# Pooled attention and expert routing: scores on all 128 rows, token ranks by a running sum

## The chip, the core and the metric

The kernel runs on one core of a Trainium2 chip. The core has a matrix engine (TensorE, PE in the profile; its weight loads are listed apart as PEld), a vector engine (VectorE, DVE), an engine for activation functions (ScalarE, ACT), a general-purpose one (GpSimd, POOL) and a queue for synchronisation and transfers (SyncE, SP). Each runs its own list of instructions in order and waits on semaphores for the others. Sixteen DMA engines move data between HBM and the on-chip memory SBUF; TensorE writes its results to PSUM, from where VectorE or ScalarE copies them out.

The metric is the device time of one execution, in microseconds (us), as the median of several runs.

## The reference: what is computed

```python
# q, k, v: (8, 8, 576, 64) float32 -- batch, heads, sequence, head size
k_p = k.reshape(B, H, Sp, 8, D).mean(axis=3)         # Sp = 576 / 8 = 72
v_p = v.reshape(B, H, Sp, 8, D).mean(axis=3)
scores = q @ k_p.T / sqrt(64)                        # 576 x 72 for each head
attn = softmax(scores)
x = (attn @ v_p), heads side by side                 # 4608 tokens x 512

for e in range(8):                                   # experts
    mask = domain_id == e                            # one expert for each token
    out[mask] = relu(x[mask] @ w1[e]) @ w2[e]        # 512 -> 1024 -> 512
```

## The kernel before

**Stages.** Attention comes first, in four pairs of batches. A pair has 16 heads (two batches of eight) and nine blocks of 128 tokens. After it come the experts, one after the other, each on the tokens routed to it. Every expert has room for 640 tokens (`CAP`); tokens beyond that go to an overflow loop at the end, which runs zero or more times (`nblk`).

**One pair of batches.** The loads of q, k and v (`load_pair`, L104) are DMAs issued by GpSimd that turn float32 into float16. All twelve stand in one software queue, in the order k, q, v of a pair. For a pair, `kp_units` pools k by matmuls with the identity (L432), copies the sums out, turns them with TensorE (L440) and copies the result to `kpT`. A head is 64 elements deep, so pooled k fills 64 rows; `kpT` holds it twice, in its lower and in its upper 64 rows. `qt_units` turns q in the same way (L495), in units of eight chunks of two tokens, into `qT`: even tokens lie in its lower 64 rows, odd ones in its upper. `vp_units` pools v (L461, L477).

`sc_unit` (L502) makes the scores of one head. Two matmuls (L515), one for each half of the rows (even and odd tokens), write two PSUM banks of a buffer, and one exponential on ScalarE (L518) takes both to `at`. For heads 46 to 63 two more matmuls (L511, "fill") are issued first: identity times some columns of `qT`, into the part of the PSUM buffer that nobody reads. `av_unit` (L521) multiplies `at` with pooled v for one block of 128 tokens (L535); VectorE divides by the sum of the exponentials (L539, L540) into `x_sb`.

**Order.** What runs when in the attention stage is written by hand: `plan` is a list of (time, unit), where one unit of time is one head's scores, and pair `pr` begins at 16 `pr`. It is sorted and issued in that order, so that TensorE's order is fixed. The scores of a head stand at each whole number; the pooling, turning and av units are spread between them with `put`.

**Writing x and gathering it.** After three av units, three blocks of x go to `x_lin` in HBM by a DMA of SyncE (L554). Those of pairs 0 to 2 are held back: `x_rows` first issues a small DMA that reads the last loaded v (`gate`, L559), and SyncE does not go on before that v is there. From `x_lin` the tokens of an expert are gathered by row numbers (`gather`, L598), a GpSimd DMA. The first three gathers of experts 0 and 1 need only the tokens of pairs 0 to 2. On GpSimd's queue stand, in this order: three gathers for expert 0, its w2, three gathers for expert 1, its w1 and its w2.

**Routing.** Which row of an expert's list a token takes is its rank among the tokens of its expert. The one-hot matrix `oh` (L193) has, for each of 36 columns of 128 tokens, eight entries for the experts. `rank_mm` (L204) makes the ranks on TensorE: one matmul with `Ls`, a strictly triangular matrix, counts inside a column, and 35 matmuls with a matrix of ones add the counts of each column to all later ones (L211). `rank_post` makes ranks, an overflow flag `ovf` and the slot from it. `ovf_mm` (L244) does the same 36 matmuls for the flags, `slot_post` (L253) uses them. The number of overflowing tokens is counted in the expert stage: `count_a` and `count_mm` (L279) in expert 2, with a PSUM buffer of kind `small`, and `count_b` (L281) in expert 3, which reads that buffer first.

**Experts.** `l1_units` is the first layer (L648, eight units), `l2_units` the second (L664, up to five), `turn_units` turns gathered rows (L612). `one(i)` gives the PSUM buffer of a second-layer unit: `small` (two buffers) for two of three, `wide` for the third. `hidden` and `paced` tie the gathers to the progress of the first layer. The output rows are scattered by GpSimd DMAs (L673).

Of the kernel before, what the change touches and what calls it, by code (L numbers as in the profile page):

```python
# [39 lines left out]
def kernel(  # L40
# [70 lines left out]
    with tc.manual_schedule():  # L111
# [5 lines left out]
        for t in xg:  # L117
            nc.vector.memzero(t[:].rearrange("p j d -> p (j d)"))
        kt, vt, qt_ = {}, {}, {}
        kt[0] = load_pair(k, 0, "k")  # L120
# [27 lines left out]
        Ls = rt.tile([128, 128], F16, name="Ls")  # L148
        nc.vector.tensor_scalar(out=Ls[:], in0=iota_f[:], scalar1=col_f[:, 0:1], scalar2=None,
                                op0=ALU.is_gt)  # L150
# [21 lines left out]
        for cc in range(NC_):  # L172
# [3 lines left out]
            if cc >= 4:  # L176
# [16 lines left out]
        oh = rt.tile([128, NCH + 1, E], F16, name="oh")  # L193
        nc.vector.memzero(oh[:, NCH, :])
        nc.vector.tensor_tensor(oh[:, 0:NCH, :], dom[:].unsqueeze(2).to_broadcast([128, NCH, E]),
                                iota_f[:, 0:8].unsqueeze(1).to_broadcast([128, NCH, E]),
                                op=ALU.is_equal)
        blk_h = blk_i = c0 = gap = mrow = mt = nblk_f = nblk_i = nov = nov_f = novp = od = ork = ovf = ovf_h = ovs = pos_h = pos_i = rank = rk = rkv = slot_i = slotf = tmp = None
# [5 lines left out]
        def rank_mm():  # L204
            nonlocal rk
            rk = small()
            nc.tensor.matmul(rk[:, 0:8 * (NCH + 1)], Ls[:], oh[:].rearrange("p c e -> p (c e)"),
                             start=True, stop=False)
            for c in range(NCH - 1):
                c1 = NCH + 1 if c < EPAIR * NC_ else NCH  # L210
                nc.tensor.matmul(rk[:, 8 * (c + 1):8 * c1].rearrange("p (c e) -> p c e", e=E), ones[:],  # L211
                                 oh[:, c, :].unsqueeze(1).to_broadcast([128, c1 - c - 1, E]),
                                 start=False, stop=(c == NCH - 2))

        def rank_post():
            nonlocal c0, gap, ovf, ovf_h, rank, rkv, slotf, tmp
            rkv = rk[:, 0:8 * NCH].rearrange("p (c e) -> p c e", e=E)

            gap = rt.tile([128, E], F32, name="gap")
            nc.vector.memzero(gap[:])  # L220
            nc.vector.tensor_scalar(out=gap[:, 0:NEARLY], in0=rk[:, 8 * NCH:8 * NCH + NEARLY],
                                    scalar1=-1.0, scalar2=float(EARLY), op0=ALU.mult, op1=ALU.add)
            nc.vector.tensor_scalar(out=gap[:, 0:NEARLY], in0=gap[:, 0:NEARLY], scalar1=0.0,
                                    scalar2=None, op0=ALU.max)
            tmp = rt.tile([128, NCH, E], F32, name="tmp")
            c0 = EPAIR * NC_
            nc.vector.tensor_copy(tmp[:, 0:c0], rkv[:, 0:c0])
            nc.vector.tensor_tensor(tmp[:, c0:NCH], rkv[:, c0:NCH],
                                    gap[:].unsqueeze(1).to_broadcast([128, NCH - c0, E]), op=ALU.add)
            nc.vector.tensor_tensor(tmp[:], tmp[:], oh[:, 0:NCH, :], op=ALU.mult)  # L230
            rank = const.tile([128, NCH], F32, name="rank")
            nc.vector.tensor_reduce(out=rank[:], in_=tmp[:], op=ALU.add, axis=AX.X)
            ovf = const.tile([128, NCH], F32, name="ovf")
            nc.vector.tensor_scalar(out=ovf[:], in0=rank[:], scalar1=float(CAP), scalar2=None,
                                    op0=ALU.is_ge)
            slotf = rt.tile([128, NCH], F32, name="slotf")
            nc.vector.tensor_scalar(out=slotf[:], in0=dom[:], scalar1=float(CAP), scalar2=None,
                                    op0=ALU.mult)
            nc.vector.tensor_tensor(slotf[:], slotf[:], rank[:], op=ALU.add)

            ovf_h = rt.tile([128, NCH], F16, name="ovf_h")
            nc.vector.tensor_copy(ovf_h[:], ovf[:])

        def ovf_mm():  # L244
            nonlocal ork
            ork = small()
            nc.tensor.matmul(ork[:, 0:NCH], Ls[:], ovf_h[:], start=True, stop=False)
            for c in range(NCH - 1):
                nc.tensor.matmul(ork[:, c + 1:NCH], ones[:],
                                 ovf_h[:, c:c + 1].to_broadcast([128, NCH - 1 - c]),  # L250
                                 start=False, stop=(c == NCH - 2))

        def slot_post():  # L253
            nonlocal od, slot_i

            od = const.tile([128, NCH], F32, name="od")
            nc.vector.tensor_scalar(out=od[:], in0=ork[:, 0:NCH], scalar1=float(NBLK * 128),
                                    scalar2=None, op0=ALU.add)
            nc.vector.tensor_tensor(od[:], od[:], slotf[:], op=ALU.subtract)
            nc.vector.tensor_tensor(od[:], od[:], ovf[:], op=ALU.mult)  # L260
            nc.vector.tensor_tensor(od[:], od[:], slotf[:], op=ALU.add)
            slot_i = const.tile([128, NCH], I32, name="slot_i")
            nc.vector.tensor_copy(slot_i[:], od[:])

        def count_a():
            nonlocal nov, ovs
            v = Later()

            nov = const.tile([128, 2], F16, name="nov")
            ovs = const.tile([128, 1], F32, name="ovs")  # L270
            v.tensor_reduce(out=ovs[:], in_=ovf[:], op=ALU.add, axis=AX.X)
            v.tensor_copy(nov[:, 0:1], ovs[:])
            v.tensor_copy(nov[:, 1:2], ovs[:])
            return v.units

        def count_mm():
            nonlocal novp
            novp = small()
            nc.tensor.matmul(novp[:, 0:2], ones[:], nov[:], start=True, stop=True)  # L279

        def count_b():  # L281
            nonlocal mrow, mt, nblk_f, nblk_i, nov_f
            v = Later()
            nov_f = const.tile([128, 1], F32, name="nov_f")
            v.tensor_copy(nov_f[:], novp[:, 0:1])
# [127 lines left out]
        def kp_units(pr):  # L413
# [3 lines left out]
            kpT = wk.tile([128, 16, 72], F16, tag="kpT", bufs=2, name="kpT")  # L417
# [3 lines left out]
            def evac(dst, src):  # L421
                if pr == 0:
                    nc.scalar.activation(dst, src, AFT.Copy)
                else:
                    nc.vector.tensor_copy(dst, src)

            def pool(w0, w1, t0):
                if t0 == 0:
                    box[w0] = small()
                pv = box[w0][:, 0:64 * (w1 - w0)].rearrange("p (w d) -> p w d", d=64)  # L430
                for t in range(t0, t0 + 4):
                    nc.tensor.matmul(pv, ident[:], kk[:, t, w0:w1, :], start=(t == 0), stop=(t == 7))  # L432
                if t0 == 4:
                    evac(kps[:, w0:w1, :], pv)

            def turn(w0, w1):
                p = small16()
                for w in range(w0, w1):
                    for half in range(2):
                        nc.tensor.transpose(p[64 * half:64 * half + 64, w - w0, :], kps[:, w, :], ident[:])  # L440
                evac(kpT[:].rearrange("p b (w g) -> p w b g", g=8)[:, w0:w1],
                     p[:, 0:w1 - w0, :].rearrange("p w (b g) -> p w b g", g=8))
# [43 lines left out]
        def qt_units(pr):  # L486
# [5 lines left out]
            def unit(j0, n, i):  # L492
# [3 lines left out]
                if i == 1 or (pr == 0 and i == 3):  # L496
                    nc.scalar.activation(qT[:, j0:j0 + n, :], p[:, 0:n, :], AFT.Copy)  # L497
                else:
                    nc.vector.tensor_copy(qT[:, j0:j0 + n, :], p[:, 0:n, :])  # L499
            return [lambda i=i: unit(8 * i, 8 if i < 4 else 4, i) for i in range(5)]  # L500

        def sc_unit(pr, bh, fill):  # L502
# [5 lines left out]
            for par in range(2):  # L508
                if fill:

                    nc.tensor.matmul(p[:, par, 288:512], ident[:],  # L511
                                     s["qT"][:, 0:2, :].rearrange("p a b -> p (a b)")[:, 0:224],
                                     start=True, stop=True, skip_group_check=True)
            for par in range(2):
                nc.tensor.matmul(p[0:72, par, 0:288], s["kpT"][64 * par:64 * par + 64, bh, :],  # L515
                                 s["qT"][64 * par:64 * par + 64, :, 8 * bh:8 * bh + 8],
                                 start=True, stop=True)
# [183 lines left out]
        for pr in range(NP):  # L701
            t0 = 16.0 * pr
            for h in range(16):
                plan.append((t0 + h, -1, lambda pr=pr, h=h: sc_unit(pr, h, 16 * pr + h >= 46)))
# [82 lines left out]
        for e in range(2, E):  # L787
# [6 lines left out]
            run(merge(u, count_a() + [count_mm] if e == 2 else count_b() if e == 3 else []))  # L794
# [120 lines left out]
```

## Time and profile before

| | |
|---|---|
| median of 14 runs | 257.42 us (256.56 to 259.58) |
| profiled execution | 256.22 us |
| its span in the profile | 254.5 us |
| TensorE busy | 228.3 us (90% of the span) |
| VectorE busy | 122.9 us (48%) |
| ScalarE busy | 92.4 us (36%) |
| GpSimd busy | 117.2 us (46%) |
| moved by DMA | 50.22 MB, 197 GB/s on average |
| first score matmul / last | 19.9 us / 89.9 us |

A busy TensorE is not TensorE at its peak: matmuls overlap one another, and the end of one is modelled. The profile names instructions by engine and line. L515, for instance, is the line of the score matmuls; "64\*72 64x288" says that the stationary matrix has 64 rows and 72 columns and that 288 columns of 64 rows stream past it. The page gives the span in 40 slices of 6.36 us; a digit is the busy share of a slice in tenths, and in the row PEclk the share of full speed that TensorE's clock was granted.

### The profile page before, as it was taken

To read this page: it belongs to the slowest core of one execution; us is meant where nothing else is said; L and a number is where in the kernel's file an instruction comes from. 1 tells how busy PE (TensorE), PEld (TensorE's weight loads), DVE (VectorE), ACT (ScalarE), POOL (GpSimd) and SP (SyncE) were. 2 spreads that over 40 slices of the span, in tenths; PEclk is the share of its full clock that TensorE was granted. 3 is DMA by queue.
4 is the path that set the end of the run, shared out by engine and by line. 5 is a ranking of instruction groups with operands and counts; after the bars stand their busy time and mean duration, and the time that the engine had idled before them with its cause. 6 is when DMAs were issued, how large, how long until landed. Compare 5 with 4: busy or idle time off the path is not lost.

```text
span 254.5 us, 5101 instructions
## 1 busy us (share of the span) xinstructions
PE 228.3 (90%) x2084; PEld 145.7 (57%) x2084; DVE 122.9 (48%) x280; ACT 92.4 (36%) x153; POOL 117.2 (46%) x157
## 2 busy tenths in 40 slices
PE   0687989999998979889989989999999999999990
PEld 0565666676666545456745745756755656656640
DVE  7356499697788662324433333532343332343320
ACT  2056747877775726132312301312302312303210
POOL 8001423030000382386846665676676767653042
PEclk9997799999999988999999999999999999999997
DMA  5999999999999299999989969949979969942032
GB/s 101 210 219 214 219 214 217 217 216 213 216 252 405 84 177 236 237 279 183 180 254 199 229 176 206 248 139 160 247 210 194 248 160 201 247 176 106 0 112 92
DMA packets 21373, 50.22 MB, mean 197 GB/s; under 512 B 2334, under 2 KB 10592, under 8 KB 19938
## 3 DMA queue, kind: packets, MB, share of 16 engines
q0 software_dynamic: 19536, 45.10, 83.3%
q1 hardware_dynamic: 1810, 4.76, 4.8%
q8 instruction: 17, 0.28, 0.4%
q14 instruction: 10, 0.08, 0.1%
HBM read 67.15 MB, written 15.20 MB: 324 GB/s over the span
## 4 chain that ended last, share of the span: by engine, by line
PE 53%; DMA 19%; issue 10%; DVE 7%; POOL 6%; ACT 2%; POOLq 1%; DVEq 0%
PE big L648 14%; PE small L664 14%; DMA v<-in_v_dram 7%; DMA v<-in_moe_w_dram 5%; DMA xg<-x_lin,xrow 5%; PE wide L648 5%; PE small L461 4%; POOL out_dram L673 4%; PE wide L664 3%; PE big L515 2%; DVE x_sb L540 2%; PE turn L612 2%; DVE qT L499 2%; PE small L432 2%; POOL xg L598 2%
## 5 line engine op out<-in xcount | busy, mean ns | idle before, releaser
L598 POOL DMA_INDIRECT xg<-x_lin,xrow x40 | 41.5, 1038 | 48.3 <-DVE rcp L539 32.3
L673 POOL DMA_INDIRECT out_dram<-y,tok x40 | 40.3, 1006 | 44.6 <-ACT y L671 18.4
L664 PEld LDWEIGHTS <-hT 128*128 128x128 f16 x272 | 25.9, 98 | 28.2 <-issue 1.6
L518 ACT ACTIVATE at<-big 72x576 f16<-72x576 f32 x45 | 28.7, 644 | 13.0 <-PE big L515 12.3
L654 DVE TENSOR_SCALAR hT<-big 128x640 f16<-128x640 f32 (+1 forms) x24 | 17.4, 724 | 31.9 <-PE big L648 25.7
L671 ACT ACTIVATE y<-small 128x512 f32<-128x512 f32 x16 | 9.6, 597 | 52.7 <-PE small L664 49.8
L652 ACT ACTIVATE hT<-big 128x640 f16<-128x640 f32 (+1 forms) x24 | 15.0, 623 | 32.1 <-PE big L648 32.1
L669 DVE COPY y<-small 128x512 f32<-128x512 f32 x16 | 11.1, 691 | 28.4 <-PE small L664 27.5
L648 PEld LDWEIGHTS <-v 128*128 128x128 f16 x192 | 18.7, 98 | 9.9 <-DMA v<-in_moe_w_dram 2.2
L648 PEld LDWEIGHTS <-k 128*128 128x128 f16 x192 | 18.9, 99 | 8.7 <-issue 1.4
L613 DVE COPY xT<-turn 128x1024 f16<-128x1024 f16 (+1 forms) x24 | 14.3, 597 | 19.1 <-PE turn L612 19.1
L648 PE MATMUL big<-xT,v 128*128 128x320 f16 (+2 forms) x144 | 21.6, 299 | 1.7 <-DMA v<-in_moe_w_dram 1.7
L648 PE MATMUL big<-xT,k 128*128 128x320 f16 (+2 forms) x140 | 21.6, 304 | 0.0
L664 PE MATMUL small<-q,hT 128*128 128x512 f16 x80 | 18.6, 379 | 0.0
L664 PE MATMUL small<-k,hT 128*128 128x512 f16 x80 | 18.4, 379 | 0.0
L664 PE MATMUL small<-v,hT 128*128 128x512 f16 x64 | 14.9, 379 | 1.2 <-DVE y L669 0.8
L535 PEld LDWEIGHTS <-at 72*128 72x128 f16 (+1 forms) x320 | 13.2, 102 | 4.8 <-ACT at L518 0.7
L515 PE MATMUL big<-qT,kpT 64*72 64x288 f16 x90 | 14.5, 318 | 1.3 <-ACT qT L497 0.8
L540 DVE TENSOR_TENSOR x_sb<-big,rcp 128x512 f16<-128x512 f32 x22 | 15.2, 691 | 0.8
L648 PEld LDWEIGHTS <-q 128*128 128x128 f16 x128 | 12.4, 98 | 5.2
L612 PEld LDWEIGHTS <-xg 128*128 128x128 f16 x160 | 10.6, 98 | 7.8 <-DMA xg<-x_lin,xrow 2.8
L612 PE MATMUL turn<-ident,xg 128*128 128x128 f16 x160 | 13.1, 219 | 1.9 <-DMA xg<-x_lin,xrow 1.9
(156 smaller groups left out, 340.1 us busy)
## 6 DMA issues: line engine op xcount, KB each, us to landing
k<-in_moe_w_dram POOLq DMA_DIRECT2D x6, 1024.0 KB, 11.7
q<-in_moe_w_dram POOLq DMA_DIRECT2D x5, 1024.0 KB, 10.9
v<-in_moe_w_dram POOLq DMA_DIRECT2D x5, 1024.0 KB, 11.5
k<-in_k_dram POOLq DMA_DIRECT2D x4, 1152.0 KB, 24.7
v<-in_v_dram POOLq DMA_DIRECT2D x4, 1152.0 KB, 26.2
x_lin<-x_sb SPq DMA_DIRECT2D x12, 384.0 KB, 6.7
q<-in_q_dram POOLq DMA_DIRECT2D x3, 1152.0 KB, 27.0
q<-in_q_dram POOLq DMA_DIRECT2D x1, 768.0 KB, 12.0
```

The costliest lines, as they stand in the source:

```text
L515: nc.tensor.matmul(p[0:72, par, 0:288], s["kpT"][64 * par:64 * par + 64, bh, :], s["qT"][64 * par:64 * par + 64, :, 8 * bh:8 * bh + 8], st ...
L518: nc.scalar.activation(at[0:72, bh % 8, :].rearrange("p (a c) -> p a c", a=2), p[0:72, :, 0:288], AFT.Exp, scale=1.0 / 64.0)
L535: nc.tensor.matmul(pv[r0:r0 + z - a, h, 0:65], s["at", bt][0:72, h, a:z], s["vp"][0:72, 8 * bt + h, :], start=True, stop=True, skip_group_ ...
L540: nc.vector.tensor_tensor(out=x_sb.rearrange("p (h d) -> p h d", d=D), in0=pv[:, :, 0:64], in1=rcp[:].unsqueeze(2).to_broadcast([128, 8, D ...
L598: i = nc.gpsimd.indirect_dma_start(out=xg[e % 2][:, j, :], out_offset=None, in_=x_lin[0:rows, :], in_offset=bass.IndirectOffsetOnAxis(ap=x ...
L612: nc.tensor.transpose(p[:, j - a, kk, :], xg[e % 2][:, j, 128 * kk:128 * kk + 128], ident[:])
L613: nc.vector.tensor_copy(xts[e][:, :, 128 * a:128 * z].rearrange("p k (j c) -> p j k c", c=128), p[:, 0:z - a])
L648: nc.tensor.matmul(p[:, a, 0:m], w1[:, kk, 128 * fi:128 * fi + 128], xT[:, kk, s0 + m * a:s0 + m * a + m], start=(kk == 0), stop=(kk == 3))
L652: nc.scalar.activation(dst, p[:, 0:nh, 0:m], AFT.Relu)
L654: nc.vector.tensor_scalar(out=dst, in0=p[:, 0:nh, 0:m], scalar1=0.0, scalar2=None, op0=ALU.max)
L664: nc.tensor.matmul(p, hT[:, fi, 128 * j:128 * j + 128], w2[:, fi, :], start=(fi == 0), stop=(fi == 7))
L673: i = nc.gpsimd.indirect_dma_start(out=out, out_offset=bass.IndirectOffsetOnAxis(ap=orig[0][:, bl:bl + 1], axis=0), in_=y[:], in_offset=No ...
```

## The change

There are four parts.

1. *Scores on 128 rows.* `kpT` is replaced by `kz`, two fixed buffers that hold a pair's pooled k twice: in the first half the lower 64 rows are filled, in the second the upper 64, and the other rows are zero. They are zeroed once, at the start, by VectorE. A score matmul now takes all 128 rows of `kz` and of `qT`. The copy into it is made in two halves, the lower one by VectorE and the upper one by ScalarE, in every pair (before, ScalarE made the whole copy in pair 0 and VectorE in the others). The fill matmuls are gone.
2. *Ranks.* `Ls` becomes `Lm`, minus one on and below the diagonal. One matmul with it and one with ones give, for each column and expert, minus the number of tokens from this row on and the column's total. A running sum along the columns (`tensor_tensor_scan`, with `cut` to start anew for each expert) turns the totals into counts up to and including each column; the two are added. `oh` is now ordered by expert, then column. The flags' ranks are made the same way.
3. *Count.* The last element of the flags' running sum is the number of overflowing tokens. `count_a`, `count_mm` and `count_b` become one `count`, only on VectorE, in expert 2.
4. *q of pair 0.* The last 12 chunks are turned as 6 and 6 instead of 8 and 4; ScalarE copies the fifth unit instead of the fourth.

```diff
+        kz = [wk.tile([128, 2, 16, 72], F16, tag="kz", bufs=2, name="kz") for i in range(2)]
+        for t in kz:
+            nc.vector.memzero(t[:].rearrange("p a b c -> p (a b c)"))
         kt[0] = load_pair(k, 0, "k")
...
-        Ls = rt.tile([128, 128], F16, name="Ls")
-        nc.vector.tensor_scalar(out=Ls[:], in0=iota_f[:], scalar1=col_f[:, 0:1], scalar2=None,
-                                op0=ALU.is_gt)
+        Lm = rt.tile([128, 128], F16, name="Lm")
+        nc.vector.tensor_scalar(out=Lm[:], in0=iota_f[:], scalar1=col_f[:, 0:1], scalar2=-1.0,
+                                op0=ALU.is_le, op1=ALU.mult)
+        cut = rt.tile([128, E, NCH], F32, name="cut")
+        nc.vector.memset(cut[:], 1.0)
+        nc.vector.memset(cut[:, :, 0:1], 0.0)
...
         def rank_mm():
-            rk = small()
-            nc.tensor.matmul(rk[:, 0:8 * (NCH + 1)], Ls[:], oh[:].rearrange("p c e -> p (c e)"),
-                             start=True, stop=False)
-            for c in range(NCH - 1):
-                c1 = NCH + 1 if c < EPAIR * NC_ else NCH
-                nc.tensor.matmul(rk[:, 8 * (c + 1):8 * c1].rearrange("p (c e) -> p c e", e=E), ones[:],
-                                 oh[:, c, :].unsqueeze(1).to_broadcast([128, c1 - c - 1, E]),
-                                 start=False, stop=(c == NCH - 2))
+            rk = small(), small()
+            for t, w in zip(rk, (Lm, ones)):
+                nc.tensor.matmul(t[:, 0:E * NCH], w[:], oh[:].rearrange("p e c -> p (e c)"),
+                                 start=True, stop=True)
...
+            run_ = rt.tile([128, E, NCH], F32, name="run_")
+            nc.vector.tensor_tensor_scan(run_[:].rearrange("p e c -> p (e c)"),
+                                         cut[:].rearrange("p e c -> p (e c)"), rk[1][:, 0:E * NCH], 0.0,
+                                         op0=ALU.mult, op1=ALU.add)
...
         def ovf_mm():
-            nc.tensor.matmul(ork[:, 0:NCH], Ls[:], ovf_h[:], start=True, stop=False)
-            for c in range(NCH - 1):
-                nc.tensor.matmul(ork[:, c + 1:NCH], ones[:],
-                                 ovf_h[:, c:c + 1].to_broadcast([128, NCH - 1 - c]),
-                                 start=False, stop=(c == NCH - 2))
+            for i, w in enumerate((Lm, ones)):
+                nc.tensor.matmul(ork[:, NCH * i:NCH * i + NCH], w[:], ovf_h[:], start=True, stop=True,
+                                 skip_group_check=True)
         def slot_post():
+            orun = rt.tile([128, NCH], F32, name="orun")
+            nc.vector.tensor_tensor_scan(orun[:], cut[:, 0, :], ork[:, NCH:2 * NCH], 0.0,
+                                         op0=ALU.mult, op1=ALU.add)
+            nov_f = const.tile([128, 1], F32, name="nov_f")
+            nc.vector.tensor_copy(nov_f[:], orun[:, NCH - 1:NCH])
...
-        def count_mm():
-            novp = small()
-            nc.tensor.matmul(novp[:, 0:2], ones[:], nov[:], start=True, stop=True)
-        def count_b():
-            v.tensor_copy(nov_f[:], novp[:, 0:1])
...
-            kpT = wk.tile([128, 16, 72], F16, tag="kpT", bufs=2, name="kpT")
+            kpT = kz[pr % 2]
...
-                evac(kpT[:].rearrange("p b (w g) -> p w b g", g=8)[:, w0:w1],
-                     p[:, 0:w1 - w0, :].rearrange("p w (b g) -> p w b g", g=8))
+                for i, act in ((0, False), (1, True)):
+                    q = slice(64 * i, 64 * i + 64)
+                    evac(kpT[q, i].rearrange("p b (w g) -> p w b g", g=8)[:, w0:w1],
+                         p[q, 0:w1 - w0, :].rearrange("p w (b g) -> p w b g", g=8), act)
...
-                if i == 1 or (pr == 0 and i == 3):
+                if i == 1 or (pr == 0 and i == 4):
...
-            return [lambda i=i: unit(8 * i, 8 if i < 4 else 4, i) for i in range(5)]
+            if pr == 0:
+                cuts = (0, 8, 16, 24, 30, 36)
+            else:
+                cuts = (0, 8, 16, 24, 32, 36)
+            return [lambda i=i: unit(cuts[i], cuts[i + 1] - cuts[i], i) for i in range(5)]
...
-                if fill:
-                    nc.tensor.matmul(p[:, par, 288:512], ident[:],
-                                     s["qT"][:, 0:2, :].rearrange("p a b -> p (a b)")[:, 0:224],
-                                     start=True, stop=True, skip_group_check=True)
-            for par in range(2):
-                nc.tensor.matmul(p[0:72, par, 0:288], s["kpT"][64 * par:64 * par + 64, bh, :],
-                                 s["qT"][64 * par:64 * par + 64, :, 8 * bh:8 * bh + 8],
-                                 start=True, stop=True)
+                nc.tensor.matmul(p[0:72, par, 0:288], s["kpT"][:, par, bh, :],
+                                 s["qT"][:, :, 8 * bh:8 * bh + 8], start=True, stop=True)
...
-            run(merge(u, count_a() + [count_mm] if e == 2 else count_b() if e == 3 else []))
+            run(merge(u, count() if e == 2 else []))
```

## The prediction

> **What bounds the kernel now.** I read the page's slices first, then the chain of waits, then the windows around the places that the chain names, and last the order of instructions on TensorE there. The page:
>
> ```profile
> PE   0687989999998979889989989999999999999990
> ...
> PEclk9997799999999988999999999999999999999997
> DMA  5999999999999299999989969949979969942032
> ```
>
> TensorE and the DMA engines are both full nearly everywhere, so the question is which is late at which point. DMA has one real hole, slice 13 (83 to 89 us), and it is free after 220 us. The chain, in order of time (start, duration, what):
>
> ```profile
> 4.59 17.69 DMA v<-in_v_dram
> ...
> 81.43 3.94 DMA x_lin<-x_sb
> ...
> 95.05 13.88 DMA v<-in_moe_w_dram
> ...
> 120.62 10.10 DMA xg<-x_lin,xrow
> ...
> 146.13 1.74 PE small L664 x8
> ...
> 157.44 2.17 PE big L648 x16
> ...
> 166.14 3.45 PE small L664 x16
> ...
> 175.89 2.17 PE big L648 x16
> ```
>
> Up to 131 us the long steps are DMA: the first v load (until 22.3), the last x write of pair 2 (until 85.4), the w1 load of expert 1 (until 108.9), a gather (until 130.8). From there on it is matmul after matmul.
>
> The attention stage between the first two is TensorE running behind the loads. The twelve q/k/v loads stand in one queue and land one after the other. Adding issue time and time to landing of the DMA view gives k1 27.1, q1 32.7, v1 38.1, k2 44.5, q2 50.0, v2 55.4, k3 60.9, q3 66.4, v3 71.8 us: one each 5.5 us, whatever TensorE does. The last, issued at 46.76:
>
> ```profile
> v<-in_v_dram POOLq DMA_DIRECT2D x1, 1152.0 KB, 25.0
> ```
>
> First uses by TensorE are 30.1, 36.1, 42.6, 48.3, 52.9, 59.5, 65.1, 69.7 and 75.5 us. So TensorE runs 2.9 to 4.5 us behind DMA, 3.7 at v3, and **no saving on TensorE can pull this stage forward by more than that**. The x writes start only when v3 is in (the gate row, at 71.8 us). From there DMA is full again until the last x write is nearly out (window, busy us and count of each engine, clock, DMA share, GB/s):
>
> ```profile
> 83.00:84.00 1.00, 1.00 (x14) 0.55 (x15) 0.86 (x2) 0.65 (x1) 0.00 (x0) 1.00 0.59 237
> 84.00:85.00 1.00, 1.00 (x10) 0.44 (x8) 0.65 (x3) 0.89 (x2) 0.00 (x0) 1.00 0.15 47
> ```
>
> The rows from 72 to 83 all have a share of 0.97 to 1.15.
>
> **Scores.** Before, two 64-row matmuls run side by side in the two halves of the array; after, two 128-row matmuls run one behind the other. The timeline shows what surrounds a pair:
>
> ```profile
> 42.03 0.43 PE L535 MATMUL wide<-vp,at 72*128 72x65 f16 x8
> ...
> 42.39 0.31 PE L515 MATMUL big<-qT,kpT 64*72 64x288 f16 x2
> ...
> 42.97 0.31 PE L515 MATMUL big<-qT,kpT 64*72 64x288 f16 x2
> ...
> 43.21 0.40 PE L461 MATMUL small<-ident,v 128*128 128x128 f16 x4
> ...
> 43.49 0.43 PE L535 MATMUL wide<-vp,at 72*128 72x65 f16 x8
> ...
> 43.76 0.61 PE L461 MATMUL small<-ident,v 128*128 128x128 f16 x8
> ```
>
> Eight av matmuls followed by full-array work take 43.49 to 43.76, 0.27 us; followed by a score pair, 42.03 to 42.39, 0.36. Entering the pair costs 0.09. From the pair's start to the next start it is 42.97 to 43.21, 0.24. A pair thus holds TensorE for 0.33 us. Its columns explain 0.12: the pooling matmuls of 320 columns (L432) follow each other at about 0.135, so 288 columns take 0.12. The rest is the change of mode. After: 2 x 0.12 = 0.24, and nothing on entry or exit if the weight loads hide, as they do for the av matmuls (eight loads and matmuls in 0.27). I take 0.24, a saving of 0.09. Bounds: 0.46, if neither load hides (106 ns each in their row), to 0.24.
>
> Here a rule speaks against the change. The Trainium skill, TensorEngine Tiling (Array Packing), Theoretical Speedup, gives up to twice the speed for a contraction of at most 64 rows; by it each pair loses 0.12, 64 pairs +7.7 us of TensorE. The same page, Key Properties, says that a change of tiling mode, not of tile, drains the engine. Here almost every pair stands alone between full-array work, and the row charges the drains with 0.21 of 0.33 us. I take the row: 64 x 0.09 = 5.8 us less, except that the five pairs at half clock (22.3 to 28.8 us) gain nothing.
>
> The fills (L511) of heads 46 to 63 go too. Fill to pair is 84.00 to 84.30 and pair to next fill 84.30 to 84.55 in the timeline, 0.54 a head, against 0.24 after: 0.30 x 18 = 5.4 us.
>
> How much arrives? Up to v3's first use 38 pairs at full clock save 38 x 0.09 = 3.4 and three filled ones 0.9: 4.3, where DMA allows 3.7. ScalarE gives some back: of each kpT copy one half moves to it while VectorE's half costs what the whole did (0.49 and 0.41; lanes are parallel), so VectorE gains nothing and ScalarE gets about 1.2 us (its own kpT row in pair 0, x2) in each of pairs 1 to 3. It is busy for about 13 of 16.8 us a pair; queued behind are exponentials (0.65), and TensorE waits for their PSUM. I leave 2.5 to 3.7 us at v3. Five more fills (1.5 us) go before the last av of pair 2, so its x_sb is ready at 76 to 78 instead of 81.4.
>
> There DMA takes over. If that write is queued by 80, the 0.59 + 0.15 us left after 83.0 are finished at 83.75; traffic ended somewhere in 84.2 to 85.0 before and landing was 85.37, so landing comes at 84.1 to 84.9: **1.0 us** (0.5 to 1.3). POOL's three gathers, w2 of expert 0, three gathers and w1 of expert 1 follow back to back from 86.4 and move with it. Next, the first x write of pair 3 (issued at 89.06, 0.98 us of DMA at 400 GB/s) falls into the hole, since its av runs 4 to 5 us earlier: another **1.0 us** (0 to 1.5) off the stream, which is saturated from 90 to 131 (shares 0.98 to 1.18), so w1 of expert 1 and the gather at 130.77 come 2.0 earlier. TensorE idles 1.68 us before 108.98 and 1.25 before 130.77, so it can follow.
>
> Now TensorE will stand still some 4 us before the first gather (attention done near 85, landing near 89.4). The clock row first: after the idle 91.9 to 94 the clock fell to half until about 97, and after the thin stretch before 22.3 it was 0.50 until 28.8. The Trainium skill, TensorE: Matmul & The Clock Gate, Part 1, has an idle window of about 3.4 us halve it, until a busy one. By the row 3 us cold are paid already; by the rule, a stop of 4 us makes it two windows, 1.7 us more in expert 0. Its work from 89.4 is 0.45 + 0.25 (turns) + 1.9 (five av) + 5.2 (L648) + 5.2 + 0.7 (L664 and turns) = 13.7 us, with 6.8 us cold +3.4: done at 106.5, still ahead of w1 at 106.9. I charge nothing.
>
> **Counting the overflow.** This part is small in the diff and lies where TensorE alone is the bound. count_mm takes one of the two `small` PSUM buffers at 144.86, and it is read only in the next expert:
>
> ```profile
> 148.64 1.89 PE L664 MATMUL small<-v,hT 128*128 128x512 f16 x8 [0.78 <-DVE y L669]
> ...
> 158.09 0.15 DVE L100 COPY nov_f<-small 128x1 f32<-128x1 f32 x1
> ```
>
> With one buffer left, expert 2's second layer waits for its own copies. By the chain rows above it takes 146.13 to 157.44, 11.31 us; expert 3's 166.14 to 175.89, 9.75. After, nov_f comes from the running sum and no buffer is held: **1.56 us**, with the matmul 1.6. Nine VectorE operations of about 0.17 us in expert 2 instead of 3 and 7 lie beside matmuls (VectorE is under 40% busy). Weights of expert 4 land some 10 us before use.
>
> **Start.** Rank: 36 matmuls, 8.78 to 12.8, become two (0.41 and 0.12): -3.5. Overflow rank: 1.0 to 0.2. Added on VectorE ahead of them: two zeroings of 1152 words, 1.12 x 1152/1280 = 1.0 each, and `cut` about 0.25, so the one-hot is done near 11.0 instead of 8.7. No row shows the running sum; nearest is the 288-element TENSOR_TENSOR at 0.46, at best that, at worst twice: 0.9. Net, the pooling of k starts about 1.1 us earlier (k landed at 10.4), and slot_post 0.8 on top. All of it ends in the wait for v at 22.32, which grows from 0.74 to about 2.7 us: **0**. Without that cover it would be 1.9. The split q chunks (12 as 6+6 instead of 8+4, a copy of about 0.8 on ScalarE starting later) are within 0.2 either way under the same wait.
>
> **Sum.** 1.0 + 1.0 + 1.6 = 3.6 us. The profiled execution took 256.22 (span 254.5 and 1.7 around it): 252.6. The median of the runs is 1.2 above it: 257.42 - 3.6 = **253.8 us**, likely 252.3 to 255.2.
>
> **Rivals.**
> *DMA hides the whole front* (0.18): landing at 85.4 as before because the writes drain late, or ScalarE's extra copies eat the lead. Only the count stays: 257.4 - 1.6 = 255.8. For it: the share near 1 up to 83. Against: the hole after it.
> *TensorE's saving gets through* (0.12): w1 of expert 1 no longer binds and expert 0's end does: gathers moved by 1.2 and no cold stretch give 104.5 instead of 108.98, 4.4 in front, 6.0 in all: 251.4. Against: w1 is DMA-bound.
> *The weight loads of the padded pairs don't hide* (0.08): 0.46 a pair, 0.13 more than now. Until the last av of pair 2, 43 pairs lose 5.6, eight filled ones gain 8 x 0.08 = 0.6: x_sb at 86.4, landing 2.1 later (the fastest x write) at 88.5, 3.1 late; less 1.6, 258.9. It decides from about 0.45 a pair. For it: the two loads alternate with no third buffer in sight. Against: the hidden loads of the av rows.
> *Without fills the clock halves in pair 3 and stays so through expert 0* (0.05): past 17 us cold after 89.4 the start of expert 1 slips over 111.8 and eats the count's gain; wholly cold it gives about 260. Against: padded pairs are full-array work.
>
> **Numbers.** Forecast 0.57, the rivals as above. What a measurement tells from no change is about 0.3%, 0.8 us. Faster by more: forecast, the third way, and most of the hidden front, 0.82; within: 0.09; slower: 0.09. The range 251.5 to 257.2 leaves out the slower cases and the end of the best.
>
> **What would show it.** L515 with 128 rows and 0.24 from start to next start; no idle before it. v3's first use near 72 to 73; last x write landing near 84.4; w1 of expert 1 used near 107; gather before expert 2 near 128.8. Expert 2's second layer at 9.75. The wait for v at 22.3 unchanged in time. I am wrong if v3 is used no earlier than 75, or if the x write lands early and w1 does not.

## The result and the profile after

| | before | after |
|---|---|---|
| median | 257.13 us (47 runs, 255.87 to 259.58) | 255.02 us (10 runs, 253.44 to 255.64) |
| profiled execution, span | 256.22, 254.5 us | 254.80, 253.1 us |
| TensorE, VectorE, ScalarE busy | 228.3, 122.9, 92.4 us | 219.6, 126.3, 94.5 us |

The ratio is 0.9907, with a 95% interval of 0.9882 to 0.9932: 2.1 us faster by the medians, 1.4 by the two profiled executions, where 3.6 were forecast. Here and below a median is over all runs, while a ratio leaves out the few executions that were over 1.5% slower than the fastest of the same kernel. The slices of the page, in tenths:

```profile
PE   0287779998987769989979999999999999999990
...
PEclk9999999999999977999999999999999999999999
DMA  5999999999999389999979979969969959942032
```

TensorE has lost 8.7 us of work, and its row shows it: in the attention stage (up to slice 13) 7s stand where 8s and 9s stood. The DMA row has not moved. The chain of waits of the changed kernel (start, duration, what), at the places where the prediction read it before:

```profile
80.64 4.90 DMA x_lin<-x_sb
...
87.94 3.58 DMA xg<-x_lin,xrow
...
95.21 13.64 DMA v<-in_moe_w_dram
108.90 1.47 PE big L639 x8
...
120.54 10.62 DMA xg<-x_lin,xrow
...
146.48 3.45 PE small L655 x16
...
156.23 2.17 PE big L639 x16
```

The last x write of pair 2 starts 0.8 us earlier and lands at 85.54, 0.2 later than before. Expert 1 starts at 108.90 (108.98 before), and the gather for expert 2, forecast to end 2.0 us earlier, ends at 131.2, 0.4 later than before. Then comes the count: expert 2's second layer takes 146.48 to 156.23, 9.75 us in place of 11.31. Less what the late gather took, expert 3 starts 1.21 us earlier than before. Nearly all of the span's 1.4 us is there. The stages in front, from which 2.0 us were forecast, show nothing.

The scores themselves are as forecast. Two pairs of the changed kernel's timeline, one behind the other:

```profile
82.37 0.42 PE L507 MATMUL big<-qT,kz 128*72 128x288 f16 x2
82.62 0.41 PE L507 MATMUL wide<-qT,kz 128*72 128x288 f16 x2
```

From start to next start it is 0.25 us, with 128 rows. Entering a pair from eight av matmuls costs nothing more:

```profile
46.87 0.43 PE L526 MATMUL big<-vp,at 72*128 72x65 f16 x8
47.14 0.41 PE L507 MATMUL wide<-qT,kz 128*72 128x288 f16 x2
```

That is 0.27 us, where it was 0.36 ahead of a 64-row pair. What reached v3 is another matter: it is first used at 75.42, before at 75.48.

### The profile page after: what moved, and what is told of

Read it like the earlier page. It is cut to its first block, busy times and chain, and to the rows that moved or that the text cites. A ratio compares the mean times of both kernels' runs of the same rounds, so it can differ in the third digit from the quotient of the medians.

```text
span 253.1 us, 4896 instructions
## 1 busy us (share of the span) xinstructions
PE 219.6 (87%) x1979; PEld 146.1 (58%) x1979; DVE 126.3 (50%) x283; ACT 94.5 (37%) x159; POOL 117.2 (46%) x157
## 4 chain that ended last, share of the span: by engine, by line
PE 49%; DMA 13%; DVE 13%; issue 10%; ACT 7%; POOL 5%; POOLq 1%; DVEq 0%; ACTq 0%
PE big L639 14%; PE small L655 14%; DMA xg<-x_lin,xrow 6%; DMA v<-in_moe_w_dram 5%; PE wide L639 5%; ACT at L509 4%; POOL out_dram L664 4%; PE wide L655 3%; DVE x_sb L531 3%; PE small L424 3%; PE turn L603 2%; DVE qT L493 2%; DMA x_lin<-x_sb 2%; PE small L489 2%; PE big L507 2%
## 5 line engine op out<-in xcount | busy, mean ns | idle before, releaser
L507 PE MATMUL big<-qT,kz 128*72 128x288 f16 x90 | 18.3, 287 | 2.5 <-DVE qT L493 1.1
L526 PEld LDWEIGHTS <-at 72*128 72x128 f16 (+1 forms) x320 | 14.8, 104 | 5.9 <-issue 2.6
```

The costliest lines, as they stand in the source:

```text
L507: nc.tensor.matmul(p[0:72, par, 0:288], s["kpT"][:, par, bh, :], s["qT"][:, :, 8 * bh:8 * bh + 8], start=True, stop=True)
L526: nc.tensor.matmul(pv[r0:r0 + z - a, h, 0:65], s["at", bt][0:72, h, a:z], s["vp"][0:72, 8 * bt + h, :], start=True, stop=True, skip_group_ ...
```

## The experiments

Each ratio is to the kernel before, run on the same chip in the same set. The intervals are some 0.3% to either side, so that two kernels are told apart only where they differ by about half a per cent. No run leaves out any part of the computation; where a run adds matmuls to keep TensorE warm, nobody reads their results.

### One part at a time

**The count alone.** The kernel before, with one more column in the overflow matmuls, whose value is the number of overflowing tokens.

```diff
-            for c in range(NCH - 1):
-                nc.tensor.matmul(ork[:, c + 1:NCH], ones[:],
...
+            for c in range(NCH):
+                nc.tensor.matmul(ork[:, c + 1:NCH + 1], ones[:],
...
+            nc.vector.tensor_copy(nov_f[:], ork[:, NCH:NCH + 1])
...
-            run(merge(u, count_a() + [count_mm] if e == 2 else count_b() if e == 3 else []))
+            run(merge(u, count() if e == 2 else []))
```

> The kernel before with only the count changed: the overflow matmuls get one more column and one more matmul, whose result is the number of overflowing tokens; no PSUM buffer is held from expert 2 to expert 3. Theory (the count gives the whole gain, the front is bound by DMA): the second layer of expert 2 takes 9.75 us as in the changed kernel instead of 11.31, and the ratio to before is 0.990 to 0.994, that of the full change within its interval. Rival (scores and ranks bring part of it): the same 9.75 us, but the full change stays ahead of this kernel by 0.5 us or more.

Measured: 0.9939 (0.9910 to 0.9969), 256.23 us where the kernel before took 257.69. Its chain of waits around expert 2's second layer:

```profile
145.86 3.45 PE small L648 x16
...
155.61 2.17 PE big L632 x16
```

9.75 us again. In the kernel before, TensorE stood for 1.24 of the 11.31 us, in two waits for copies that free the other `small` buffer; in the changed kernel it stands for nothing there. So the PSUM buffer held by the count accounts for the 1.56: 1.24 in the waits, and 0.3 in longer matmul records around them.

**All but the count.** The changed kernel with `count_a`, `count_mm` and `count_b` of before.

```diff
-            run(merge(u, count() if e == 2 else []))
+            run(merge(u, count_a() + [count_mm] if e == 2 else count_b() if e == 3 else []))
```

> The changed kernel with the count of before put back (two column sums, a matmul into a held PSUM buffer, its reading in expert 3). Theory (count only): expert 2's second layer at about 11.3 us again and the ratio to before within 0.002 of 1. Rival (front brings part): ratio 0.996 to 0.998, about 0.7 us of gain left.

Measured: 0.9963 (0.9942 to 0.9984), 256.53 us. Expert 2's second layer takes 11.30 us (146.85 to 158.15), and both waits are back:

```profile
149.34 1.89 PE L670 MATMUL small<-v,hT 128*128 128x512 f16 x8 [0.78 <-DVE y L675]
...
156.26 1.89 PE L670 MATMUL small<-v,hT 128*128 128x512 f16 x8 [0.46 <-ACT y L677]
```

The interval leaves out 1, as the rival had it: a little is left without the count, 0.2 to 0.6%.

**Scores undone.** The changed kernel with `kpT`, its undivided copy, 64-row pairs and fills. With `kz` the two zeroings at the start go too.

```diff
-                nc.tensor.matmul(p[0:72, par, 0:288], s["kpT"][:, par, bh, :],
-                                 s["qT"][:, :, 8 * bh:8 * bh + 8], start=True, stop=True)
+                nc.tensor.matmul(p[0:72, par, 0:288], s["kpT"][64 * par:64 * par + 64, bh, :],
+                                 s["qT"][64 * par:64 * par + 64, :, 8 * bh:8 * bh + 8],
...
```

> The changed kernel with the score part put back: 64-row pairs side by side, fills for heads 46 to 63, one undivided copy of turned k. Theory (front bound by DMA): same time as the full change within 0.3 us, w1 of expert 1 used near 108.9 us as in both kernels. Rival (padding brings part): slower than the full change by 0.7 us. Rival (padding costs, by its divided copies): faster than the full change by 0.5 us or more.

Measured: 0.9924 (0.9894 to 0.9954), 256.24 us, which cannot be told from the changed kernel. v3 is first used at 72.68, **2.7 us earlier** than with the padded scores, and expert 1 starts at 108.08. Nearly all of the 2.7 us is there at the first score already (19.60 instead of 22.23): it is the zeroings that are missing, not the padding.

**Ranks undone.** The changed kernel with the 36 rank matmuls of before, and the count from the extra column.

```diff
-            for t, w in zip(rk, (Lm, ones)):
...
+            for c in range(NCH - 1):
...
+                nc.tensor.matmul(rk[:, 8 * (c + 1):8 * c1].rearrange("p (c e) -> p c e", e=E), ones[:],
...
```

> The changed scores, count and q chunks with the 36 rank matmuls of before. Theory (these matmuls raised TensorE's clock ahead of the pooling of k): the 16 pooling matmuls of pair 0 take 2.1 us as before instead of 4.0, the first scores start before v lands, at 20 to 21 us instead of 22.2, and the end moves by less than 0.3 us since DMA decides it. Rival (the pooling took 4.0 us because of PSUM buffers held by the ranks, not of the clock): the single pooling matmuls keep their distance of 0.13 us in the changed kernel but wait once in the middle; undoing the ranks then also gives 2.1 us.

Measured: 0.9947 (0.9921 to 0.9973), 256.38 us. The pooling of k takes 2.60 us. That the first score would come at 20 to 21 us was a miss: it comes at 23.42, since the 36 matmuls themselves take 4.60 us behind the zeroings, and v3 at 77.22.

**The changed kernel and the count alone, side by side,** five rounds each:

> The changed kernel again, unedited, beside the next run on the same chip. Theory (the stages ahead of the experts bring a little through pair 2's last av and the start of expert 1): ratio to the kernel before 0.990 to 0.992, and 0.2 to 0.4% (0.5 to 1.0 us) below the kernel that has the new count alone. Rival (only the count is worth anything): the two ratios lie within 0.15% of each other.

> The kernel before with the new count alone, again. Theory: ratio 0.993 to 0.995, so that 0.2 to 0.4% of the change's gain is left to the padded scores. Rival: the same ratio as the changed kernel within 0.15%, and the padded scores bring nothing that can be measured.

Measured: the changed kernel 0.9934 (0.9908 to 0.9960), 255.25 us; the count alone 0.9922 (0.9900 to 0.9945), 255.44 us. The rival holds: **side by side, nothing beyond the count can be measured.** The changed kernel without the count, 0.4% faster with an interval that leaves out 1, speaks for a small rest. Between nothing and 0.6% it stays open.

### Does it matter when attention is done?

Every run has its own first use of v3, so the profiles together answer this. Ten of fourteen follow; the other four have v3 at 74.8 to 74.9 us and the first gather at 86.1 to 86.7. The columns are starts in us: the first score, v3's first use, the first gather, GpSimd's issue of expert 1's w1 where the chain names it, and the start of expert 1.

| kernel | first score | v3 used | first gather | w1 issued | expert 1 |
|---|---|---|---|---|---|
| scores undone | 19.60 | 72.68 | 86.41 | - | 108.08 |
| count alone | 20.70 | 73.59 | 86.10 | 94.79 | 108.43 |
| warm start (below) | 20.39 | 73.79 | 86.76 | 95.41 | 108.41 |
| count alone, again | 21.01 | 73.89 | 86.65 | 95.31 | 109.41 |
| copies by buffer (below) | 22.21 | 74.75 | 86.46 | 95.13 | 108.79 |
| changed kernel | 22.23 | 75.42 | 86.55 | 95.21 | 108.90 |
| before | 19.92 | 75.48 | 86.38 | 95.05 | 108.98 |
| changed kernel, again | 22.33 | 75.52 | 86.38 | 95.04 | 108.47 |
| ranks undone | 23.42 | 77.22 | 86.05 | - | 109.99 |
| three edits (below) | 25.94 | 78.48 | 87.03 | 95.70 | 110.58 |

v3's first use moves over 5.8 us, the first gather over 1.0, and not in step with it. From there to w1's issue it is 8.65 to 8.69 us in every row that has both. So an earlier end of attention buys nothing at the gathers. For the start of expert 1, one profile tells little below 1 us: the count alone has 108.43 and 109.41. But a late end costs: with v3 after 77, expert 1 starts at 110.0 and 110.6, behind all the others of the table. Why the gather stays shows in the windows of the changed kernel (window, busy us and count of PE, PEld, DVE, ACT and POOL, clock, DMA share, GB/s):

```profile
83.00:84.00 1.00, 0.82 (x11) 0.54 (x10) 0.64 (x4) 1.00 (x3) 0.00 (x0) 1.00 0.69 273
84.00:85.00 1.00, 0.80 (x11) 0.52 (x10) 0.89 (x2) 1.00 (x3) 0.00 (x0) 1.00 0.14 55
```

Before, these rows had 0.59 and 0.15. The same traffic is still on its way, although x was ready sooner. The write that is ready earlier waits in the DMA engines: ready at 79.49 with the warm start it landed after 6.26 us, ready at 81.43 before after 3.94. TensorE does not set when this traffic begins. The gate on v3 does, at 71.80 us before and here at

```profile
71.97 0.31 SPq L550 DMA_DIRECT2D gate<-v  x1
```

and from 72 to 83 us the DMA share of the changed kernel is 0.99 to 1.13 in every row.

### Where the padded scores' lead went

The row of v3 above splits in two. The first score is 2.31 us later than before, and the stretch from there to v3 is 53.19 us instead of 55.56. But with the count alone, with 64-row pairs, that stretch is 52.88: the kernel before ran at half clock from 22.0 to 28.8 us, which no other profile here shows (in its runs of the later sets the mean granted clock is 0.977 to 0.980, that of the changed kernel 0.976 to 0.979). With only the scores undone it is 53.08. At full clock the padded pairs bring the stretch nothing. TensorE's busy time in it is less (47.09 us, against 48.51 with the scores undone and 49.23 with the count alone), and its waits are as much longer. The waits of the changed kernel in this stretch (who waits for whom: us, times, longest) name the new ones:

```profile
ACT kz L415 <- DVE kz L417: 2.9, 6, 0.9
...
PE small L489 <- ACT kz L415: 1.5, 3, 1.0
```

and its timeline shows one of them:

```profile
68.04 0.48 DVE L417 COPY kz<-small 64x640 f16<-64x640 f16 x1 [0.23 <-PE small L432]
68.56 0.70 ACT L415 ACTIVATE kz<-small 64x640 f16<-64x640 f16 x1 [0.28 <-DVE kz L417]
...
69.31 0.61 PE L489 MATMUL small<-ident,q 128*128 128x128 f16 x8 [0.23 <-ACT kz L415]
```

The two halves of the copy read one PSUM buffer, and ScalarE's starts when VectorE's has ended. TensorE gets its buffer back after 1.2 us; before, after one copy of 0.49. The next run gives each buffer's two halves to one engine:

```diff
-                for i, act in ((0, False), (1, True)):
+                for i, act in ((0, w0 > 0), (1, w0 > 0)):
```

> The changed kernel with the copies of turned k divided by buffer and not by rows: VectorE copies both halves of the first buffer, ScalarE both of the second. In the changed kernel ScalarE's copy began only when VectorE's of the same buffer had ended (3.6 us of waiting in seven places). Theory (these waits eat TensorE's lead, but the lead is not what ends the front): the turning of q after them starts 0.3 to 0.7 us earlier in each pair, and the time stays within 0.4 us. Rival (TensorE's lead counts): 0.7 us or more faster.

Measured: 0.9879 (0.9835 to 0.9923), 254.22 us from 6 runs. The stretch fell from 53.19 to 52.54 us, so the copies cost some 0.65 of it; the five other profiles with the changed kernel's start and copies have 53.14 to 53.20.

### The start

The pooling of k takes 4.00 us in the changed kernel and took 2.12 before, for the same sixteen matmuls. The next run adds 22 matmuls around the rank matmuls (warm start):

```diff
+        spin(14)
         rank_mm()
+        spin(8)
```

> The changed kernel with 22 unread matmuls around the rank matmuls, some 3 us of TensorE work, so that it is as busy there as in the kernel before. Theory (the pooling of k runs at half rate because the 36 removed matmuls no longer come ahead of it): its 16 matmuls take 2.1 to 2.7 us in place of 4.00; the end of the kernel unchanged within 0.2% of the changed kernel. Rival (it is slow because it shares buffers with the ranks): 3.5 us or more again.

Measured: 0.9927 (0.9897 to 0.9958), 255.47 us. The timeline's line for the changed kernel, and then for this one:

```profile
12.18 4.00 PE L424 MATMUL small<-k,ident 128*128 128x320 f16 x16 [0.84 <-DVE run__193 L223]
```

```profile
12.19 2.16 PE L424 MATMUL small<-k,ident 128*128 128x320 f16 x16
```

The pooling is at full speed again, as it nearly was with the ranks undone (2.60), so the removed rank matmuls had kept TensorE warm. v3 came 1.6 us earlier, and the time did not change: which shows the front's slack once more.

The start is late for another reason. TensorE's first matmul comes at 7.74 us instead of 5.80, because two lines stand before it in VectorE's timeline of the changed kernel:

```profile
3.86 1.02 DVE L123 MEMSET kz<- 128x1152 uint32 x1 [0.19 <-issue]
5.07 1.02 DVE L123 MEMSET kz<- 128x1152 uint32 x1 [0.19 <-issue]
```

### Using the hole, and the clock

**w2 of expert 0 into the DMA hole at 83 to 89 us,** on GpSimd ahead of the gathers:

```diff
-        put(wload_units(0, 1, 1), 57.1, 57.1)
+        def w2_early():
+            nc.gpsimd.tensor_copy(mark[:], st[2]["x"][0:1, 2, 0:1])
+            wload_units(0, 1, 1)[0]()
+        put([w2_early], 53.5, 53.5)
```

> The changed kernel with one transfer moved: the load of w2 of expert 0 is issued when the last x of pair 2 is ready (about 81 us) and so before the gathers, not after the first three. Theory (from 84 to 131 us the kernel is bound by the DMA stream and its hole at 84 to 88): the hole fills, w1 of expert 1 lands near 105 instead of 108.9, expert 1 then starts when expert 0 is done (107 to 108), and the wait of 1.8 us before the turn near 131 is gone: 1.5 to 3 us faster than the changed kernel, about 252.5. Rival (the x writes in flight share the engines with w2): they land 2 us or more later, the gathers slip, and the time is the same or worse.

Measured: 0.9994 (0.9967 to 1.0022), 257.33 us: the gain of the change was lost. Its chain of waits:

```profile
80.13 5.03 DMA x_lin<-x_sb
...
87.49 5.66 DMA xg<-x_lin,xrow
...
121.29 12.28 DMA xg<-x_lin,xrow
...
134.33 2.83 PE small L655 x8
```

The write is not held up, but the gather behind w2 takes 5.66 us instead of 3.58. Later the DMA engines stand half idle (share 0.48 and 0.62 from 110 to 120 us, against 1.15 and 1.01), and the gather for expert 2 ends 2.4 us later, at 133.6. After that wait TensorE runs at half clock from 134.8 to 138.2 (the last row: 2.83 us where the changed kernel takes 1.73), so that expert 3 starts at 160.30, 4.1 us later. The profiled run, 259.02 us, is the slowest of the 14. The hole has only moved: from 86 to 131 us the DMA engines follow a chain of gathers, an expert and the next loads, and are not one full stream.

**Twelve unread matmuls before the first turn,** to keep TensorE warm:

```diff
+        def warm():
+            p = small()
+            for i in range(12):
+                nc.tensor.matmul(p[:], ident[:], st[3]["qT"][:, 0:4, :].rearrange("p a b -> p (a b)"),
...
+        put([warm], 63.9, 63.9)
```

> The changed kernel with 12 matmuls of 512 columns (result unread) on TensorE between the last scores and the turn that waits for the first gather. Theory: the clock does not fall to half at 92 us, expert 0 is done 2 us earlier, but w1 of expert 1 still lands near 108.9, so expert 1 starts then and the time is within 0.4 us of the changed kernel. Rival (the half clock in expert 0 is what holds the front): 1.5 us or more faster.

Measured: 0.9867 (0.9825 to 0.9908), 254.03 us from 6 runs. Half clock is left from 93.9 to 97.3 us only; in the changed kernel it was 91.6 to 98.4.

**Both together:**

```diff
+        put([w2_early], 53.5, 53.5)
...
+        put([warm], 63.9, 63.9)
```

> Both of the two edits before. Theory: each removes one of two limits that end together near 108 us, so that together they give more than the sum: expert 1 starts at 105 to 106, 3 to 4 us faster than the changed kernel, about 251. Rival: no more than the moved load alone.

Measured: 0.9958 (0.9933 to 0.9983), 256.23 us, a miss where about 251 was expected; the gathers behind w2 took 5.62 us again.

**Copies by buffer, warm matmuls, and the zeroing on GpSimd,** meant as the best of all:

```diff
-            nc.vector.memzero(t[:].rearrange("p a b c -> p (a b c)"))
...
+            nc.gpsimd.memset(t[:].rearrange("p a b c -> p (a b c)"), 0.0)
```

> The changed kernel with three edits: the copies of the turned k divided by buffer, twelve unread matmuls ahead of the first turn, and the zeroing of the two padded buffers on GpSimd. Theory (gains in different stages add up): the warm matmuls and the divided copies were each worth 0.2 to 0.4%, so the ratio is 0.984 to 0.987, 253.3 to 254.0 us. Rival (expert 1 waits for its first weights at 108.4 to 108.8 whatever comes ahead of it): no better than the warm matmuls alone, 0.987 or above.

Measured: 0.9993 (0.9973 to 1.0013), 256.75 us, worse than either theory. The timeline shows why, first on VectorE, then on GpSimd:

```profile
4.86 5.98 DVE L150 TENSOR_SCALAR ident<-iota_f,col_f 128x128 f16<-128x128 f32 x1
...
6.69 4.07 POOL L141 MEMSET kz<- 128x2304 f16 x2
```

VectorE's operation, of 0.28 us in the changed kernel, ends at 10.84, just after GpSimd's zeroing at 10.76. TensorE starts 4 us later than in the changed kernel, and v3 at 78.48 is past the slack. The Trainium skill, SBUF — State Buffer, "SBUF: two separate sides", says that GpSimd and VectorE, in some of its operations, share a port pair which one instruction holds exclusively; the common end agrees, though no run shows that this operation is one of them. What held VectorE from 4.86 to 6.69, before the zeroing, no run shows: GpSimd was issuing loads then, but beside the same loads the operation took 0.37 us in the kernel before.

The warm matmuls alone and the divided copies alone have the lowest times, 254.0 and 254.2 us. They did not run beside the changed kernel (0.9907 in one set, 0.9934 in another), so whether they beat it is open.

## Why the prediction was right in sign and too large

Of the three terms, 1.6, 1.0 and 1.0 us, the first came for the stated reason, and the other two measured nothing. That 255.02 us lies well within the range of 251.5 to 257.2 is in part luck: the range was wide enough to hold the rival with the hidden front as well.

- **The count** (1.6 us forecast). This was right: 1.56 us in the trace, and 0.6 to 0.8% when it is made alone. It carries the result.
- **A padded pair** (0.24 us instead of 0.33). Right. The row, not the rule on packing, gave the better answer: TensorE lost work.
- **2.5 to 3.7 us at v3.** This failed: v3 is used 0.06 us earlier. "of each kpT copy one half moves to it while VectorE's half costs what the whole did" counted ScalarE's busy time, but not that the two halves run one behind the other on a buffer that TensorE waits for. And the forecast started from a stretch that was 2.5 to 2.7 us longer through half clock, which went away by itself and covered the late start in the sum.
- **The start at 0** ("All of it ends in the wait for v at 22.32"). Right in sum, wrong in reason. The zeroing was priced well (1.02 each, 1.0 forecast), the running sum too (0.75 us, between 0.46 and 0.9). Missed were the cold pooling (1.9 us) and the two `small` buffers held until the running sum (0.84). The cover was gone: v was in at 21.7 and first used at 23.02 (22.32 before). It cost nothing at the end, since later slack covered it, not v.
- **"the 0.59 + 0.15 us left after 83.0 are finished at 83.75": 1.0 us.** This is the step that failed in the sum. What was left was the tail of a full stream, not a write that came late. The condition, a write queued by 80, was met with the count alone (79.54 and 79.83), the copies by buffer (79.97) and the warm start (79.49), and it landed at 85.08 to 85.75, not at 84.1 to 84.9. The term measured 0.
- **The first x write of pair 3 in the hole: 1.0 us.** It did start earlier (87.57 instead of 89.06), and the DMA share from 88 to 90 rose. But the stream after it did not gain, because GpSimd issues w1 about 8.67 us after the first gather wherever the order of its queue is kept. The term measured 0.1 at expert 1, less than two profiles of one kernel differ by, and -0.4 at the gather for expert 2.
- **The longer cold stretch, charged nothing.** Right in its cost, and in its size by luck. Half clock grew from 3.4 us to 6.8, and expert 0 was still ready 0.91 us before w1. But TensorE did not stand still for 4 us; its longest wait there is 1.41 us:

```profile
91.56 0.61 PE L603 MATMUL turn<-ident,xg 128*128 128x128 f16 x4 [1.41 <-DMA xg<-x_lin,xrow]
...
108.90 1.47 PE L639 MATMUL big<-xT,v 128*128 128x384 f16 x8 [0.91 <-DMA v<-in_moe_w_dram]
```

The count alone has 6.8 us of half clock too, in both profiles, and the changed kernel, profiled again, 10.2 us, with 0.29 us left before w1. So the length was not the change's doing, and the idle window of 3.4 us that the rule on the clock asks for, as the prediction cites it, did not come before it.

- **The rivals.** "DMA hides the whole front" is what happened, by its first cause. Its own sum was 255.8; 255.02 and 255.25 were measured, and 255.5 is the kernel before in these sets (257.1) less the count's 1.6. It had been given 0.18, held down by the argument that a hole follows at 83 us. "I am wrong if v3 is used no earlier than 75" came true for the front.

## What to carry to other kernels

A hole in the DMA row shows that nothing is queued there, not that the work ahead of it came late: look at whether the rows before it are full; where they were, here, no earlier producer helped. Look for small buffers that are held over a long wait, as the count's was; here one matmul's result, kept for the next expert, was worth more than 64 pairs of scores made faster. And when a copy is divided between two engines, try dividing it by buffer rather than within one: here TensorE's stretch became 0.65 us shorter, though no gain in the whole time is shown for it.

## What had not been expected of the hardware

- The profile's clock row reads 1.00 at 12 to 16 us, where the sixteen pooling matmuls of the changed kernel took 4.00 us; with the warm start, under the same clock row, 2.16. There the row said nothing about TensorE's speed; the matmuls' durations did.
- Half clock came in stretches of 3.4, 6.8 or 10.2 us in these profiles (the kernel's end apart), and in the 3.4 us ahead of one TensorE's longest wait was 0.2 to 2.2 us: the clock fell without a stop of 3.4 us.
- VectorE's and ScalarE's copies out of one PSUM buffer ran one after the other, though they touch different partitions: ScalarE waited 2.9 us for VectorE in six places. The profile ends the wait with a semaphore of VectorE, ahead of ScalarE's instruction, which speaks for the program's own order; it was not tried apart.
- GpSimd took 4.07 us to zero the two buffers that VectorE zeroes in 1.02 each, and an operation of VectorE ended only behind it.
